# Attention and routed experts on one core: loads of q, k and v on ScalarE's queue, q without zero columns, first pair in halves, a new order

## Chip, cores, metric

One core of a Trainium2 chip. The metric is the device time of one execution in microseconds (us); lower is better. The engines are called as in the profile: PE (TensorE, matmuls; PEld its weight loads), DVE (VectorE), ACT (ScalarE), POOL (GpSimd) and SP (SyncE, which computes nothing and issues transfers).

## What is computed

```python
def rotate(x):
    x1, x2 = (x[..., :half], x[..., half:])
    return np.concatenate([x1 * cos - x2 * sin, x1 * sin + x2 * cos], axis=-1)
scores = scale * np.matmul(rotate(q), rotate(k).transpose(0, 1, 3, 2))   # q, k, v: (8, 8, 576, 64) float32
attn = np.exp(scores - np.max(scores, axis=-1, keepdims=True))
attn_out = np.matmul(attn / (np.sum(attn, axis=-1, keepdims=True) + 1e-9), v)
# x: attn_out with the 8 heads beside each other, (8, 576, 512)
scores = np.einsum('bsd,d->bs', x, w_gate)
out = x.copy()
for b in range(B):                       # 8 batches, capacity 128
    top_idx = np.argpartition(-scores[b], capacity)[:capacity]
    xe = x[b, top_idx]
    ye = np.maximum(xe @ w1, 0.0) @ w2   # w1 (512, 1024), w2 (1024, 512)
    g = 1.0 / (1.0 + np.exp(-scores[b, top_idx]))
    out[b, top_idx] = x[b, top_idx] + g[:, None] * ye
```

## The kernel before, in words

The work is cut into 32 pairs of heads, four pairs to a batch. The two heads of a pair lie on 64 partitions each. Each pair goes through these stages.

- **Load (`load`, lines 449 to 468).** One transfer each for k, q and v (lines 466 and 457), all issued by SP. The host lays k and q out with the two halves of the head dimension exchanged in a second copy, so k is 128 x 2 x 576 floats. q is 128 x 2 x 640: its last 64 columns stand twice, each time with zeros in the place of the other head, so that both heads' last rows can be one unit of matmuls (`_packed`, line 1060). k and q have one tile each, `k_in` and `q_in`; v has two, and a copy with exchanged partitions made by ACT or POOL (line 463).
- **Rotate (`rotate`, lines 470 to 506).** For k, then q: multiply by the tables of cosines and sines `tabs` (line 483), add the two copies into the one tile `turned` (line 485, one buffer for k and q alike), ACT casts the sum to the matmul's type (`kh`, `qh`, line 487), and the rest is subtracted out (`kl`, `ql`, line 488). POOL does the three element-wise steps for every pair but the first, DVE for the first.
- **Attend.** Nine units per pair (128 rows of one head; the ninth holds the last 64 rows of both). A unit: 3 products on PE (line 537: kh·qh, kl·qh, kh·ql), minimum and negation on DVE (line 558), exp on ACT (line 566), a transpose in blocks of 32 on DVE (line 589), a copy aside by ACT or POOL (line 595), transfers inside SBUF that put the halves in their places (`move`, line 621, `pt<-pt`, eight per pair; two of each four overwrite what the first two read and wait for them), and the product with v on PE (line 648). Then PE turns the rows (line 701) and ACT or DVE scales them (lines 716, 720).
- **Experts.** After four pairs SP stores the batch's rows, and `route` picks 128 of 576 rows by counting, gathers them, runs w1 and w2 on PE (line 925) and scatters them back. The weights come in 16 transfers with a cast on ACT and a subtraction on POOL (lines 987 to 991) during pairs 1 to 4.

**What sets the order.** Nothing is written out in program order. Every step is an `Op` with a key (a due time), the engines that could do it with their costs, and what it waits for. `Order.run` plays them through as a list schedule: a free engine takes the ready operation with the smallest key, and the instructions are emitted in that sequence, so each engine's stream (and SP's queue) has a fixed order that the planner believed good. `KEY` holds due times and thresholds, `SEEDS` draws small offsets for the keys, pair by pair. Urgent operations (units, softmax) may hold their engine idle up to `patience`; when PE has been less busy than `warm` of a stretch, the planner puts in idle matmuls (`L359`) that compute nothing. Transfers are planned on SP, one after the other: `moving` is the time at which the last one has passed, `size` how long each takes. The chip then runs the streams with semaphores; an engine that comes to an instruction too early waits there, and all behind it waits too.

**Start.** `tabs` is loaded whole by ACT (line 1002), then k, q and v of the first two pairs by SP.

Of the kernel before, what the change touches and what calls it, by code (L numbers as in the profile page):

```python
# [19 lines left out]
P = 128  # L20
# [3 lines left out]
KEY = dict(warm=0.72, warm0=20000, warm1=1000000, dummy=430, dcols=256, ahead=15000, lag=16000, rem=400, value=17500, rows=5250, load=29000, rotate=115700, half=2500,  # L24
           gate=10237, route=58400, count=31062, select=10850, turn=21875, step=7600, count_=20000, select_=3000, turn_=78750, step_=8550, last_step=1750, kstep=2700, hold=3,
           vcopy=6000, lift=range(9), lifted=688, patience=1400, over=600, near=-1050, swap=9750, vsplit=9, vstep=1500, recip=7500, pool_lo=1, esplit=1, t_most=4)


SEEDS = (287, 515, 547, 816, 264, 235, 869, 51, 137, 55, 51, 156, 400, 832, 65, 162, 511, 401, 998, 837, 195, 321, 307,
         523, 695, 769, 161, 691, 826, 584, 917, 834, 923)  # L30
# [14 lines left out]
class Order:  # L45
# [33 lines left out]
    def run(self):  # L79
# [23 lines left out]
        count, fetched, moving, landed = 0, 0.0, 0.0, []  # L103
# [35 lines left out]
        while events:  # L139
# [4 lines left out]
            while moved:  # L144
                moved = False
                for e in names:
# [3 lines left out]
                    while waiting[e]:  # L150
# [10 lines left out]
                        if can > t:  # L161
                            if o.urgent and can < t + KEY["patience"] and (soon is None or can < soon):
                                soon = can
                        elif soon is None or t + o.engines[e][0] <= soon + KEY["over"]:
# [109 lines left out]
def attention_moe_kernel(ctx: ExitStack, tc: tile.TileContext, q, k, v, gate, w1, w2, rope, outs, shape, cap):  # L274
# [43 lines left out]

    banks = ps.tile([P, 8, 512], F32, name="ps")
# [22 lines left out]

    T32, M512 = 109.0, 232.0
    LOAD, VALUES, WEIGHTS, STORE = {"SP": (600, 2100)}, {"SP": (600, 2050)}, {"SP": (520, 1400)}, {"SP": (600, 2200)}
# [23 lines left out]
    tabs = sb("tabs", [P, 2, REM + KW])  # L368
# [54 lines left out]
    nc.vector.memset(minus, -1.0)  # L423
    nc.gpsimd.iota(place, pattern=[[P, NT + 1]], base=0, channel_multiplier=1, allow_small_or_imprecise_dtypes=True)
# [21 lines left out]
    loaded, stacks = {}, {}  # L446
    last_first = []

    def load(pi, names="kqv", after=()):
# [3 lines left out]
        for i, (n, src, tiles) in enumerate((("k", k, k_ins), ("q", q, q_ins), ("v", v, vts))):  # L453
            if n in names:
                use = uses[n] = tiles.next()
                if n == "v":
                    o = op(VALUES, lambda src=src, use=use: nc.sync.dma_start(use.tile[:, 0], src[b, j]), key + i,
                           use.before + list(after), size=1050)
                    got[n].append(o)
                    for h in range(2):  # L460
                        mine, there = slice(64 * h, 64 * h + 64), slice(64 - 64 * h, 128 - 64 * h)
                        got[n].append(op({"ACT": act((NB // 2) * D), "POOL": pool_copy((NB // 2) * D)},
                                         lambda e, use=use, mine=mine, there=there: (nc.gpsimd.tensor_copy if e == "POOL" else nc.scalar.copy)(  # L463
                                             use.tile[mine, 1], use.tile[there, 0]), key + KEY["vcopy"], [o]))
                else:
                    got[n].append(op(LOAD, lambda src=src, use=use: nc.sync.dma_start(use.tile, src[b, j]), key + i,
                                     use.before + list(after), size=1900 if n == "k" else 2100))
                use.by(*got[n])

    def rotate(pi):  # L470
# [3 lines left out]
        key, base = at(pi, 0) - KEY["rotate"], at(pi, 0) - KEY["ahead"]  # L474
        kh, kl, qh, ql = (r.next() for r in (khs, kls, qhs, qls))
# [5 lines left out]
        def part(use, sum_use, sum_, tab, hu, lu, c0, c1, got):  # L481
            x, n = use.tile, c1 - c0
            m = op(time(2 * n), lambda: e.tensor_tensor(  # L483
                x[:, :, c0:c1], x[:, :, c0:c1], tab[:, :, c0:c1], op=ALU.mult), key, got)
            y = op(time(n), lambda: e.tensor_tensor(  # L485
                sum_[:, c0:c1], x[:, 0, c0:c1], x[:, 1, c0:c1], op=ALU.add), key, [m] + sum_use.before)
            c = op({"ACT": act(n)}, lambda: nc.scalar.copy(hu.tile[:, c0:c1], sum_[:, c0:c1]), base, [y] + hu.before)  # L487
            d = op(time(n), lambda: e.tensor_tensor(  # L488
                lu.tile[:, c0:c1], sum_[:, c0:c1], hu.tile[:, c0:c1].bitcast(F32), op=ALU.subtract), base, [c] + lu.before)
# [3 lines left out]
            return c0, c1, [c, d]  # L493

        for name, hu, lu in (("k", kh, kl), ("q", qh, ql)):
            use = uses[name]
            sum_use = turned.next()
            sum_ = sum_use.tile
            tab = tabs[:, :, 0:S] if name == "k" else tabs[:, :, REM:REM + KW]
            for c0, c1 in ((0, S),) if name == "k" else ((0, KW),) if not first else ((0, P), (P, MAIN), (MAIN, KW)):  # L500
                parts.setdefault(name, []).append(part(use, sum_use, sum_, tab, hu, lu, c0, c1, got[name] + wait))

# [619 lines left out]
```

## Time and profile before

| | us |
|---|---|
| median of 3 runs | 587.43 |
| lowest and highest | 586.22, 590.15 |
| profiled execution | 585.07 |
| its span, first to last instruction | 583.3 |

The profile is of one execution. Busy time is the time in which an engine executes; waits in an engine's own queue and the issue of a transfer by SP or ACT are not in it. A row of the timeline has start, duration, engine and line, what is written from what is read, the count, and in brackets how long the engine stood idle before it and what released it. A chain of waits is followed back from the last instruction to what released each step.

### The profile page before, as it was taken

Reading aid. Unit: us, or ns where it says so; the run is one execution under the profiler, and the core shown is the slowest. Engines: PE = TensorE matmul, PEld = TensorE weight load, DVE = VectorE, ACT = ScalarE, POOL = GpSimd, SP = SyncE. Lnnn points to the kernel's source line nnn. Section 1 sums busy time; section 2 is a strip of 40 time slices with the busy share of each in tenths; the row PEclk is TensorE's granted clock in tenths of the full one; section 3 lists DMA queues with packets and bytes.
Section 4 is the critical chain, followed back from the end, with each engine's and each line's share of the span. In section 5 each row is a group of like instructions: output and inputs, shape, how many; then the busy total and the mean of one; then the engine's idle time right before and its main releaser. Section 6 shows DMA issues by size and latency. Waiting matters only on the chain.

```text
span 583.3 us, 19385 instructions
## 1 busy us (share of the span) xinstructions
PE 523.4 (90%) x7496; PEld 434.2 (74%) x7496; DVE 495.5 (85%) x1242; ACT 477.9 (82%) x1318; POOL 452.9 (78%) x417
## 2 busy tenths in 40 slices
PE   0678889888998998999998999989889999899996
PEld 0567778677886887788877878778778778788884
DVE  6968989888989998999998998888899999899331
ACT  2759999988989988998887978898798988979321
POOL 3699999997999887897878888888799778924310
PEclk9979899998999999999999999999999999999999
DMA  5386888867787677868887677677878577645200
GB/s 216 106 236 185 241 264 231 252 179 238 197 246 197 194 215 191 219 178 220 246 198 203 157 214 195 194 196 199 238 212 224 147 217 200 181 111 136 72 31 24
DMA packets 55484, 110.83 MB, mean 190 GB/s; under 512 B 6752, under 2 KB 35808, under 8 KB 55392
## 3 DMA queue, kind: packets, MB, share of 16 engines
q1 hardware_dynamic: 53968, 104.67, 65.4%
q0 software_dynamic: 1280, 4.20, 2.2%
q8 instruction: 59, 0.97, 0.7%
q10 hardware_dynamic: 144, 0.72, 0.3%
q14 instruction: 33, 0.27, 0.1%
HBM read 56.30 MB, written 11.53 MB: 116 GB/s over the span
## 4 chain that ended last, share of the span: by engine, by line
DMA 28%; ACT 22%; POOL 17%; PE 10%; issue 10%; DVE 9%; SPq 2%; POOLq 0%; ACTq 0%; DVEq 0%
DMA pt<-pt 11%; ACT pab L566 8%; DMA q_in<-q_dram 7%; DMA vt<-v_dram 6%; ACT pt L595 4%; PE ps L648 4%; POOL turned L485 4%; POOL q_in L483 4%; DVE pt L589 4%; POOL k_in L483 3%; DVE pab L558 3%; PE ps L537 2%; ACT vt L463 2%; POOL kl L488 2%; PE ps L925 2%
## 5 line engine op out<-in xcount | busy, mean ns | idle before, releaser
L589 DVE STREAM_TRANSPOSE pt<-pab 128x576 f32<-128x576 f32 x256 | 190.3, 762 | 36.4 <-ACT pab L566 33.2
L566 ACT ACTIVATE pab<-pab,nm 128x576 f32<-128x576 f32 x256 | 196.5, 770 | 8.0 <-DVE pab L558 7.0
L558 DVE TENSOR_SCALAR_CACHE_REDUCE pab<-ps 128x576 f32<-128x576 f32 x256 | 180.6, 741 | 7.1 <-PE ps L537 6.1
L648 PE MATMUL ps<-pt,vt 64*64 64x128 f32 (+1 forms) x4608 | 159.3, 286 | 6.4 <-DVE pab L558 3.6
L648 PEld LDWEIGHTS ps<-pt,vt 64*64 64x64 f32 x4608 | 141.3, 133 | 18.9 <-issue 5.5
L537 PE MATMUL ps<-kh,qh 64*128 64x288 f32 (+1 forms) x576 | 90.0, 350 | 31.2 <-ACT qh L487 15.0
L483 POOL TENSOR_TENSOR q_in<-q_in,tabs 128x1280 f32<-128x1280 f32 x31 | 91.6, 2956 | 25.2 <-DMA q_in<-q_dram 23.2
L595 ACT COPY pt<-pt 128x288 f32<-128x288 f32 x227 | 89.9, 429 | 16.9 <-DMA pt<-pt 8.4
L537 PEld LDWEIGHTS ps<-kh,qh 64*128 64x128 f32 (+1 forms) x576 | 51.2, 189 | 69.4 <-ACT qh L487 15.4
L483 POOL TENSOR_TENSOR k_in<-k_in,tabs 128x1152 f32<-128x1152 f32 x31 | 82.7, 2667 | 10.6 <-DMA k_in<-k_dram 10.1
L537 PE MATMUL ps<-kh,ql 64*128 64x288 f32 (+1 forms) x576 | 71.8, 299 | 4.3 <-POOL ql L488 2.9
L537 PE MATMUL ps<-kl,qh 64*128 64x288 f32 (+1 forms) x576 | 71.1, 296 | 0.0
L701 PE MATMUL ps<-turner,ot 128*128 128x136 f32 x320 | 51.9, 294 | 8.3 <-ACT ot L348 5.4
L537 PEld LDWEIGHTS ps<-kh,ql 64*128 64x128 f32 (+1 forms) x576 | 54.2, 190 | 4.9 <-POOL ql L488 3.1
L701 PEld LDWEIGHTS ps<-turner,ot 128*128 128x128 f32 x320 | 43.0, 192 | 16.4 <-ACT ot L348 7.6
L537 PEld LDWEIGHTS ps<-kl,qh 64*128 64x128 f32 (+1 forms) x576 | 53.9, 190 | 0.0
L488 POOL TENSOR_TENSOR ql<-turned,qh 128x640 fp32r<-128x640 f32 x31 | 48.3, 1557 | 6.2 <-ACT qh L487 4.7
L925 PE MATMUL ps<-w,xt 128*128 128x512 f32 x192 | 52.9, 409 | 0.0
L925 PE MATMUL ps<-w,ht 128*128 128x512 f32 x192 | 51.1, 405 | 0.0
L485 POOL TENSOR_TENSOR turned<-q_in 128x640 f32<-128x640 f32 x31 | 48.3, 1558 | 1.2
L566 ACT ACTIVATION_READ_ACCUMULATOR pab<-pab,nm 128x1 f32 x256 | 48.2, 188 | 0.0
L488 POOL TENSOR_TENSOR kl<-turned,kh 128x576 fp32r<-128x576 f32 x31 | 44.1, 1423 | 2.4 <-ACT kh L487 2.1
(107 smaller groups left out, 738.6 us busy)
## 6 DMA issues: line engine op xcount, KB each, us to landing
pt<-pt SPq DMA_DIRECT2D x124, 180.0 KB, 4.4
q_in<-q_dram SPq DMA_DIRECT2D x32, 640.0 KB, 5.6
k_in<-k_dram SPq DMA_DIRECT2D x32, 576.0 KB, 6.0
pt<-pt SPq DMA_DIRECT2D x128, 144.0 KB, 3.8
vt<-v_dram SPq DMA_DIRECT2D x32, 288.0 KB, 4.1
out_dram<-x SPq DMA_DIRECT2D x16, 512.0 KB, 4.0
xe<-w_dram SPq DMA_DIRECT2D x8, 256.0 KB, 4.7
h<-w_dram SPq DMA_DIRECT2D x8, 256.0 KB, 5.4
```

Of the source, the lines that this page charges most:

```text
L463: lambda e, use=use, mine=mine, there=there: (nc.gpsimd.tensor_copy if e == "POOL" else nc.scalar.copy)(use.tile[mine, 1], use.tile[there, ...
L483: m = op(time(2 * n), lambda: e.tensor_tensor(x[:, :, c0:c1], x[:, :, c0:c1], tab[:, :, c0:c1], op=ALU.mult), key, got)
L485: y = op(time(n), lambda: e.tensor_tensor(sum_[:, c0:c1], x[:, 0, c0:c1], x[:, 1, c0:c1], op=ALU.add), key, [m] + sum_use.before)
L488: d = op(time(n), lambda: e.tensor_tensor(lu.tile[:, c0:c1], sum_[:, c0:c1], hu.tile[:, c0:c1].bitcast(F32), op=ALU.subtract), base, [c] + ...
L537: nc.tensor.matmul(bank_of(bs[i])[:, n, 0:HALF], lt, rt, start=start, stop=stop)
L558: nc.vector.tensor_scalar(halves, bank_of(b)[:, :, 0:HALF], -1.0, None, op0=ALU.mult, op1=ALU.min, accum_out=nm.tile[:, u:u + 1])
L566: lambda: nc.scalar.activation(halves, halves if lift else bank_of(b)[:, :, 0:HALF], AF.Exp, bias=nm.tile[:, u:u + 1], scale=-1.0 if lift ...
L589: nc.vector.transpose(into, src.rearrange("p (m w j) -> p m w j", w=2, j=32))
L595: (nc.gpsimd.tensor_copy if e == "POOL" else nc.scalar.copy)(apart(c)[:, to * L:to * L + L], two)
L648: nc.tensor.matmul(bank_of(acc)[64 * h:64 * h + 64, g, c0:c0 + 32 * n], vt.tile[gp_, h ^ g, (m - 1) % 2 * NT + (m - 1) // 2 if m else 2 * ...
L701: nc.tensor.matmul(bank_of(b)[:, W * i:W * i + W], ot.tile[:, i * P:i * P + P], turner, start=True, stop=True)
L925: nc.tensor.matmul(bank_of(bank), lhs.tile[:, a, c * P:c * P + P], w[w_][:, c, fs], start=(c == 0 and i == 0), stop=(c == n - 1 and i == 2))
```

## The change

- `KEY` and `SEEDS` get new values, so the whole order is another; `warm` goes from 0.72 to 0.86. Transfers are planned with other lengths, on two queues that slow each other when both move, and the moves count as urgent on SP.
- Loads of q, k and v from the second pair on, the gate and all loads of v are issued by ACT. Moves, stores and weights stay on SP.
- q is loaded as 128 x 2 x 576. The zeros stand in `q_sum` from the start; the sum of the last 64 columns is written by two more additions on 64 partitions each, between the zeros.
- `turned` becomes two tiles, `k_sum` and `q_sum`.
- For the first pair, k comes in two transfers of 288 columns, q in two of 128 and 448, the tables in three; the rotation follows in those pieces. The copy of the first v is due late and on ACT alone.

```diff
-KEY = dict(warm=0.72, ..., ahead=15000, lag=16000, value=17500, load=29000, rotate=115700,
-           route=58400, count=31062, select=10850, turn=21875, step=7600, count_=20000, turn_=78750, step_=8550, last_step=1750,
-           patience=1400, over=600, near=-1050, vstep=1500, ...)
+KEY = dict(warm=0.86, ..., ahead=15000, lag=16000, value=17500, load=30500, rotate=173549,
+           route=21900, count=23781, select=5425, turn=24609, step=11400, count_=24062, turn_=98437, step_=10820, last_step=4750,
+           patience=900, over=450, near=-900, vstep=2250, ..., ring="ACT", vring="ACT", wring="SP", issue=120,
+           svc0=800, svc1=200, svck=2101, svcq=2251, svcv=1501, first_moves=True, over_dma=750, patience_dma=1150)
...
-                    if e == "SP":
+                    if e == "SP" or e == "ACT" and o.size:
                         begin = max(begin, landed[-self.FLYING]) if len(landed) >= self.FLYING else begin
-                        moving = max(moving, begin + lasts) + o.size
-                        lasts = moving + self.LANDED - begin
+                        other = "ACT" if e == "SP" else "SP"
+                        from_ = max(moving[e], begin + lasts)
+                        both = min(o.size, max(0.0, moving[other] - from_))
+                        moving[e] = from_ + o.size + both
...
+    striped = lambda t: t[:, MAIN:KW].rearrange("p (a h j) -> p a h j", a=2, h=2)
+    ISSUE = {"SP": 420, "ACT": KEY["issue"]}
+    start_dma = lambda e: (nc.scalar if e == "ACT" else nc.sync).dma_start
-    LOAD, VALUES, ... = {"SP": (600, 2100)}, {"SP": (600, 2050)}, ...
+    LOAD, VALUES, ... = {KEY["ring"]: (ISSUE[KEY["ring"]], 1400)}, {KEY["vring"]: (ISSUE[KEY["vring"]], 1400)}, ...
...
-    q_ins = ring("q_in", 1, [P, 2, KW])
+    q_ins = ring("q_in", 1, [P, 2, S])
-    turned = ring("turned", 1, [P, KW])
+    k_sums = ring("k_sum", 1, [P, S])
+    q_sums = ring("q_sum", 1, [P, KW])
...
+    for h in range(2):
+        nc.vector.memset(striped(q_sums.tiles[0])[64 * h:64 * h + 64, :, 1 - h], 0.0)
...
+    FIRST = {"k": ((0, HALF), (HALF, S)), "q": ((0, P), (P, S))}
...
-                    got[n].append(op(LOAD, lambda src=src, use=use: nc.sync.dma_start(use.tile, src[b, j]), ...
+                elif pi:
+                    got[n].append(op(LOAD, lambda src=src, use=use: start_dma(KEY["ring"])(use.tile, src[b, j]), ...
+                else:
+                    for c, (c0, c1) in enumerate(FIRST[n]):
+                        got[n].append(op({"SP": (400, 1400)}, lambda ...: nc.sync.dma_start(
+                            use.tile[:, :, c0:c1], src[b, j, :, :, c0:c1]), ...
...
+            def add():
+                m1 = MAIN if edge else c1
+                e.tensor_tensor(sum_[:, c0:m1], x[:, 0, c0:m1], x[:, 1, c0:m1], op=ALU.add)
+                for h in range(2) if edge else ():
+                    hp = slice(64 * h, 64 * h + 64)
+                    a, b = (x[hp, i, MAIN:S].rearrange("p (a j) -> p a j", j=32) for i in range(2))
+                    e.tensor_tensor(striped(sum_)[hp, :, h], a, b, op=ALU.add)
...
-    nc.scalar.dma_start(tabs, rope)
+    cuts = (0, HALF, S, REM + S)
+    tabs_in = [op({"ACT": (400, 1400)}, lambda a=a, b=b: nc.scalar.dma_start(tabs[:, :, a:b], rope[:, :, a:b]), ...)
+               for i, (a, b) in enumerate(zip(cuts, cuts[1:]))]
...
-            load(pi + 1, "v")
+            load(pi + 1, "v", last_first[-1:] if not pi else ())
```

## Rows read from the trace of the kernel before

**Rows 1.** The page's chain that ended last, shares of the span by engine.
```profile
DMA 28%; ACT 22%; POOL 17%; PE 10%; issue 10%; DVE 9%; SPq 2%; POOLq 0%; ACTq 0%; DVEq 0%
```

**Rows 2.** By stretch: length, busy PE, PEld, DVE, ACT, POOL (instructions), clock, DMA share, GB/s.
```profile
0.00:35.00 35.00, 12.82 (x88) 10.59 (x90) 24.92 (x61) 15.78 (x35) 20.83 (x30) 0.94 0.52 171
35.00:100.00 65.00, 60.04 (x880) 49.77 (x877) 57.63 (x142) 61.32 (x167) 61.67 (x40) 0.95 0.82 231
...
535.00:583.00 48.00, 42.47 (x490) 35.99 (x486) 16.72 (x51) 15.02 (x43) 9.84 (x20) 0.97 0.20 61
35.00:535.00 500.00, 468.15 (x6928) 387.62 (x6928) 453.88 (x1132) 447.11 (x1242) 422.23 (x369) 0.99 0.75 204
```

**Rows 3.** Timeline of the first 35 us.
```profile
0.81 0.40 ACTq L1002 DMA_DIRECT2D tabs<-rope_dram  x1
...
0.81 0.38 SPq L466 DMA_DIRECT2D k_in<-k_dram  x1
...
1.25 0.42 SPq L466 DMA_DIRECT2D q_in<-q_dram  x1
...
1.71 1.07 SPq L457 DMA_DIRECT2D vt<-v_dram  x2
...
7.41 1.36 DVE L483 TENSOR_TENSOR k_in<-k_in,tabs 128x1152 f32<-128x1152 f32 x1 [4.29 <-DMA tabs<-rope_dram]
...
9.48 2.55 DVE L483 TENSOR_TENSOR q_in<-q_in,tabs 128x256 f32<-128x256 f32 x3
...
12.73 3.40 DVE L485 TENSOR_TENSOR turned<-q_in 128x384 f32<-128x384 f32 x3
...
17.55 0.76 DVE L558 TENSOR_SCALAR_CACHE_REDUCE pab<-ps 128x576 f32<-128x576 f32 x1 [0.54 <-PE ps L537]
...
20.14 2.94 POOL L483 TENSOR_TENSOR q_in<-q_in,tabs 128x1280 f32<-128x1280 f32 x1 [4.36 <-DMA q_in<-q_dram]
...
23.03 1.44 POOL L485 TENSOR_TENSOR turned<-k_in 128x576 f32<-128x576 f32 x1
...
34.11 0.76 DVE L558 TENSOR_SCALAR_CACHE_REDUCE pab<-ps 128x576 f32<-128x576 f32 x1 [3.64 <-PE ps L537]
```

**Rows 4.** Waits from 35 to 535: engine, line, released by: us, times, longest.
```profile
ACT vt L463 <- DMA vt<-v_dram: 10.6, 9, 1.9
ACT pt L595 <- DMA pt<-pt: 8.4, 7, 2.6
...
POOL q_in L483 <- DMA q_in<-q_dram: 18.8, 16, 2.7
...
POOL k_in L483 <- DMA k_in<-k_dram: 8.8, 8, 2.0
...
DVE pt L589 <- ACT pab L566: 33.2, 47, 2.0
```

**Rows 5.** Waits of SP's own queue, whole run: us, times, longest.
```profile
SPq L621 <- DMA pt<-pt: 102.2, 58, 5.7
SPq L466 <- POOL turned L485: 52.8, 26, 8.0
```

**Rows 6.** Issues of loads on SP: ns of one, minimum, median, maximum.
```profile
L466 SPq DMA_DIRECT2D q_in<-q_dram x32: 328/335/1424, 1.2 to 495.4; - x32
...
L457 SPq DMA_DIRECT2D vt<-v_dram x32: 323/526/1632, 1.7 to 521.6; - x32
```

**Rows 7.** Groups of instructions: count, busy us, mean ns, idle before.
```profile
L483 POOL TENSOR_TENSOR q_in<-q_in,tabs 128x1280 f32<-128x1280 f32 x31 | 91.6, 2956 | 25.2 <-DMA q_in<-q_dram 23.2 <-DMA vt<-v_dram 1.9
...
L483 POOL TENSOR_TENSOR k_in<-k_in,tabs 128x1152 f32<-128x1152 f32 x31 | 82.7, 2667 | 10.6 <-DMA k_in<-k_dram 10.1
...
L485 POOL TENSOR_TENSOR turned<-q_in 128x640 f32<-128x640 f32 x31 | 48.3, 1558 | 1.2
...
L359 PE MATMUL ps<-tabs,turner 128*128 128x256 f32 x128 | 35.7, 403 | 2.6 <-POOL pt L595 1.4 <-ACT gp L718 1.2
...
L786 POOL TENSOR_TENSOR gp<-gp,rs 128x40 f32<-128x40 f32 x7 | 1.9, 275 | 0.1
```

More of the change, by code (lines that the diff above doesn't have):

```diff
@@ L21 @@
 EPS = 1e-9
[L24 to L30, printed above, removed]
+KEY = dict(warm=0.86, warm0=20000, warm1=1000000, dummy=430, dcols=256, ahead=15000, lag=16000, rem=400, value=17500, rows=5250, load=30500, rotate=173549, half=2500,
+           gate=10237, route=21900, count=23781, select=5425, turn=24609, step=11400, count_=24062, select_=3000, turn_=98437, step_=10820, last_step=4750, kstep=2700, hold=3,
+           vcopy=6000, lift=range(9), lifted=688, patience=900, over=450, near=-900, swap=9750, vsplit=9, vstep=2250, recip=7500, pool_lo=1, esplit=1, t_most=4, ring="ACT", vring="ACT", wring="SP", issue=120, svc0=800, svc1=200, svck=2101, svcq=2251, svcv=1501, first_moves=True, over_dma=750, patience_dma=1150)
+SEEDS = (565, 391, 564, 144, 101, 455, 841, 8, 256, 824, 805, 812, 257, 897, 41, 772, 284, 205, 874, 236, 788, 528,
+         325, 737, 176, 896, 862, 855, 154, 898, 194, 459, 973)
 NOISE = 300.0
@@ L479, in rotate, with part @@
         parts = {}
-        def part(use, sum_use, sum_, tab, hu, lu, c0, c1, got):
+        def part(use, sum_use, sum_, tab, hu, lu, c0, c1, got, more=0):
             x, n = use.tile, c1 - c0
             m = op(time(2 * n), lambda: e.tensor_tensor(
[L484 to L487, printed above, removed]
+                x[:, :, c0:c1], x[:, :, c0:c1], tab[:, :, c0:c1], op=ALU.mult), key + more, got)
+            edge = name == "q" and c1 == S
+            def add():
[5 more added lines that the diff above has]
+                    e.tensor_tensor(striped(sum_)[hp, :, h], a, b, op=ALU.add)
+            y = op(time(n) if not edge else {"DVE": dve(n, 1, 200.0)} if first else {"POOL": pool(MAIN, 540.0)}, add, key + more, [m] + sum_use.before)
+            d1 = KW if edge else c1
+            n = d1 - c0
+            c = op({"ACT": act(n)}, lambda: nc.scalar.copy(hu.tile[:, c0:d1], sum_[:, c0:d1]), base + more, [y] + hu.before)
             d = op(time(n), lambda: e.tensor_tensor(
-                lu.tile[:, c0:c1], sum_[:, c0:c1], hu.tile[:, c0:c1].bitcast(F32), op=ALU.subtract), base, [c] + lu.before)
+                lu.tile[:, c0:d1], sum_[:, c0:d1], hu.tile[:, c0:d1].bitcast(F32), op=ALU.subtract), base + more + 3000 * first, [c] + lu.before)
             use.by(m, y), sum_use.by(y, c, d), hu.by(c, d), lu.by(d)
@@ L492, in part @@
                 last_first.append(y)
[L493 removed]
+            return c0, d1, [c, d]
+        whole = ((0, S),)
         for name, hu, lu in (("k", kh, kl), ("q", qh, ql)):
             use = uses[name]
[L497 removed]
+            sum_use = (k_sums if name == "k" else q_sums).next()
             sum_ = sum_use.tile
[L499 to L501 removed]
+            tab = tabs[:, :, 0:S] if name == "k" else tabs[:, :, REM:REM + S]
+            for i, (c0, c1) in enumerate(FIRST[name] if first else whole):
+                needs = [got[name][i]] + tabs_in[i if name == "k" else 0:i + 1 if name == "k" or not i else 3] if first else got[name] + wait
+                parts.setdefault(name, []).append(part(use, sum_use, sum_, tab, hu, lu, c0, c1, needs, first * (4000 * i + 2000 * (name == "q"))))
         def have(t):
[L504 removed]
+            return [o for x in parts["k"] for o in x[2]] + [o for c0, c1, l in parts["q"] if c0 <= t * P < c1 for o in l]
         stacks[pi] = (kh, kl, qh, ql, have)
@@ L1066, in _packed @@
     turned = x.reshape(B, H // 2, 2, S, D).transpose(0, 1, 2, 4, 3)
-    last = np.zeros((B, H // 2, 2, D, 2, 2, 32), x.dtype)
-    for h in range(2):
-        last[:, :, h, :, :, h] = turned[:, :, h][..., rest[:, 0]]
-    whole = [turned[..., rest.reshape(-1)], turned[..., main]]
-    if apart:
-        whole = [whole[1], last.reshape(B, H // 2, 2, D, -1)]
-    whole = np.concatenate(whole, -1)
+    whole = [turned[..., main], turned[..., rest]]
+    whole = np.concatenate(whole[::-1] if ahead else whole, -1)
     other = np.concatenate([whole[:, :, :, D // 2:], whole[:, :, :, :D // 2]], 3)
```

48 lines of the change are left out of this document (28 added, 20 removed).

## The prediction

> **What bounds the kernel now.** I read the chain that ended last first. No engine owns it: transfers have 28%, ACT 22%, POOL 17%, PE 10%, DVE 9% [rows 1]. The table by stretch says why. From 35 to 535 us, 500 us in which 31 pairs go by, PE is busy 468.15 us, DVE 453.88, ACT 447.11, POOL 422.23 [rows 2]. PE's figure flatters: 128 idle matmuls make 35.7 us of it [rows 7]. So three engines lie within a few per cent of each other, none is full, and the stage is bounded by DVE's 454 us at best: 46 us are lost to waits. The waits of that stage show DVE waiting 33.2 us for ACT's exp, ACT waiting 10.6 us for v and 8.4 for moved blocks, POOL waiting 18.8 us for q and 8.8 for k [rows 4]. Last I looked at SP's own queue, where those transfers come from: it stands 102.2 us in front of moves that wait for earlier moves, and 52.8 us in front of loads of k and q that wait for POOL to have read the old ones [rows 5]. A load that is ready stands behind such a move, and a move behind such a load.
>
> The ends are different. In the first 35 us DVE works 24.92, PE 12.82 and POOL 20.83 us [rows 2]. Nothing begins until the tables land at 7.41; the first softmax step is at 17.55; and DVE stands 3.64 us before the second pair goes on at 34.11, because POOL multiplied q only at 20.14 and added k only at 23.03 [rows 3]. The last 48 us are PE's, 42.47 busy, by the experts of the last batches [rows 2].
>
> **Start, in halves.** The first multiplication needs half of k and half of the tables. 704 KB of tables took from 0.81 to 7.41 beside k, q and v, the first loads of v being issued at 1.71 [rows 3]. By bytes alone half of k's columns, 288 of 704, would take 6.6 x 288/704 = 2.7 us. Whether landing goes by bytes no row shows, so the first step is 0 to 3.9 us earlier; I take 2.5, nearer the end that goes by bytes, since v now stands in ACT's stream behind the first casts and leaves the first microseconds to the others. Then DVE's path to the first unit: today k whole (1.36 for the product), q's three products 2.55, q's three sums 3.40 stand ahead of the first softmax [rows 3]. After it, of q only 128 of 640 columns must be done first: (2.55 + 3.40) x 512/640 = 4.8 us move behind it, less about 1 us in which the second half of k and of the tables is still landing. First softmax at about 17.55 - 2.5 - 3.8 = 11.3. The 4.8 us are not gone; DVE does them between units. What is gone is idle time: up to 4.29 us before 7.41 and the 3.64 before 34.11 [rows 3].
>
> For the second gap POOL's chain counts. With two sum tiles, q's sum no longer waits until k's low part is out of `turned`, and the second pair's loads no longer wait for all of the first q. From k's product to the last low part POOL needs 2.67 + 1.40 + 2.67 + 1.80 + 1.40 + 1.56 = 11.5 us (product and sum of k, the same of q, the two low parts; 576 columns as 1558 x 576/640 = 1.40, the 1.80 from below [rows 7]); begun at 12 to 13, when DVE has read the first k, it ends at 24 to 25. DVE's own work on the first pair (12.9 us from 17.55 to 34.11 - 3.64 = 30.47 [rows 3], plus the moved 4.8, all from 11.3 on) is then the later one and ends at 29. It needs 34.11 today. So 5 us, a little more with what DVE waits between its first steps today; bounds -2 (the first landing alone) and -8 (4.29 + 3.64). What it may run into: POOL is busy 61.67 of the next 65 us [rows 2], so POOL must have been released earlier too, which its own earlier start does. I take **-6**.
>
> **Loads issued by ACT.** 31 pairs by three loads. SP's issue of one takes 0.335 us for k or q and 0.526 for v in the median, 1.4 and 1.6 at most [rows 6]; ACT's one issue took 0.40 [rows 3]. If ACT can do nothing else meanwhile: 31 x (0.335 + 0.335 + 0.526) = 37 us, and ACT goes from 447 to 484 of 500 [rows 2], above DVE. If the issue runs beside an exp already started: 0. The nearest row is SP's own, but SP has no work that could cover it; ACT's waits (500 - 447 = 53 us) can. I take half as showing on ACT, 18 us, and of that ACT's share of the chain, 22% [rows 1]: **+4**, bounds 0 and +18 (484 us and the 53 - 19 = 34 us that ACT waits for other things than v and moves make 518 of today's 500). Behind a load on ACT stand the exps, and behind these DVE's transposes; the longest waits of that pair of engines already sum to 33.2 us [rows 4].
>
> The Trainium skill, "Advanced Engine Details and Errata", section "Sequencer and Instruction Queues", says that other engine instructions can be read and queued while a control instruction executes. By that the term would be 0 and the sum 4 us lower; no row here shows a load between two exps.
>
> **Waits for transfers.** With loads off SP's queue a move is held by moves alone, and a load by its buffer alone. Of the 46.6 us that ACT and POOL wait for transfers in the four largest rows (10.6 + 8.4 + 18.8 + 8.8 [rows 4]) not all can go, as the 16 engines are 75% busy in the stage and 82% in 35 to 100 [rows 2]. ACT's 19 us are nearly all on the path, POOL's 27.6 partly (it has 78 us to spare in 500). I let half of ACT's go (9.5) and a tenth of POOL's (2.8), less what comes late next, DVE, which has no more than 46 us above its own work: **-11**. Bounds 0 and -25. Two rings that move at once make each load longer; q's missing zeros give back 31 x 128 x 2 x 64 x 4 bytes = 2.0 MB, a tenth of q, which I count within this.
>
> A rule speaks against this term. The row first: from 35 to 100 us the transfer engines are 82% busy [rows 2]. "DMA: Bandwidth & Descriptors", section "Issuing engines are not separate DMA queues", of the Trainium skill says that transfers from several engines run on the same 16 engines and interleave, and that only the issue time is saved. The trace agrees in that one ring alone already reaches this share; by the rule the term is 0 (that is the second rival below).
>
> **POOL's arithmetic.** q's product shrinks from 2956 to 2667 ns [rows 7], 31 x 0.289 = -9.0 us of POOL. Its sum becomes 512 columns (1558 x 512/640 = 1.25) and two small additions, for which the nearest row is 275 ns [rows 7]: 1.80 against 1.558, +7.5 us. Net -1.5 us on an engine with 78 to spare: 0, between -1 and +2.
>
> **The rest.** More idle matmuls: each delays a real one by at most its 0.4 us [rows 7]; PE ran at a granted 0.94 and 0.95 in the first 100 us [rows 2], so some clock is won back. 0, between -3 and +3. Experts are due about two pairs earlier (route to turn sums to 75,700 against 122,200 planner ns at 20,000 a pair), which fills PE's idle gaps from 95 us on and can shorten the 48 us at the end or not: 0, between -4 and +4. The other seeds I count as noise, 0, between -5 and +5. The zeros of q's sum are two small memsets in DVE's 4.29 us wait [rows 3]: nothing, and as little if that cover goes.
>
> **Sum.** -6 + 4 - 11 + 0 = -13 on the profiled 585.07 gives 572. The profiled execution lies 2.4 us under the median of 587.43. From that median the sum gives 574.4. The terms overlap (a pair that starts earlier meets the same POOL, 61.67 of 65 us busy [rows 2]), so I take 2 off the gain: **576**.
>
> **Rivals.**
> *A, slower: ACT is held at the loads.* SP stands 52.8 us at loads of k and q, 26 times, 2.0 us each [rows 5]. On SP that costs nothing; on ACT the exps stand behind it. Where POOL is late against the planner's reckoning, the same wait falls on ACT. For it: half of 52.8 plus 18 us of issue makes ACT 447 + 44 = 491, and with its 19 us of transfer waits 510 in place of 500: +10, -6 at the start, no gain in waits, and some 5 us more that DVE waits for exps: 587.4 + 9 = 596. The stage grows from 16 us of such waits on, and from 22 us on they outweigh the start's gain. Against: the order is made anew, with the loads placed where the planner has the buffer free.
> *B, no change: the transfer waits only move.* Waits term 0, start and issue as above, -2 to 0: 585 to 587. For it: 75% busy transfer engines. Against: the 102.2 us of SP's queue.
> *C, much faster:* the issue is free and ACT's 19 us of waits go wholly, POOL's with them: 587.4 - 6 - 20 = 561. Against: DVE would stand at 95% of the stage.
> *D: the halves bring nothing*, since all pieces land together at 7.4. Then my forecast loses some 4 us: 580.
>
> **How the numbers follow.** Forecast with D inside it: 0.50, its own range 569 to 583. A 0.12, B 0.24, C 0.14. About 1% (5.9 us) is what a measurement of this kernel can tell from no change. Below 581.5 lie 0.46 of the forecast's 0.50, all of C and 0.04 of B: 0.64. Above 593.3 lies most of A: 0.10. The rest, 0.26, is within 1%. For 8 in 10 the range goes down to 563, which takes in the half of C that falls a little short, and up past B to 590; A and the rest of C, some 0.18, stay out.
>
> **What would show it.** Right: DVE's first step near 5 us, first softmax near 11, second pair's near 28; POOL's waits at q and k smaller by a third or more; the sum of ACT's waits for v and moves about halved; ACT's idle time before an exp no longer for a load's release. Wrong: exps that wait with a load issue between them (A); the same sums of waits under other names with a transfer share near 0.8 (B); POOL between 35 and 100 above 62 of 65 us with the start's gain gone by 100 us.

## The result and the profile after

The change made the kernel slower by about 1%: the ratio of after to before is 1.0115 [1.0083, 1.0148], the median of after 594.70 us against 586.73 us for before, each of 20 runs. Forecast were 576 and a range of 563 to 590. Six of after's 20 runs, the profiled one of 599.67 us (span 598.0) among them, fell in a slower state and count in the median but not in the ratio, so sums of waits in that profile may be some us high.

Line numbers of the changed kernel: units L570, minimum L591, exp L599, transpose L622, copy aside L628, moves L654, product with v L681, end of a pair L719, rotation L504 and L510/L514, casts L519, loads of k and q L481, of v L469, idle matmuls L367.

**The start.** Timeline of after, the rows that answer to [rows 3]:

```profile
5.46 0.76 DVE L504 TENSOR_TENSOR k_in<-k_in,tabs 128x576 f32<-128x576 f32 x1 [2.01 <-DMA k_in<-k_dram]
...
10.15 1.08 DVE L504 TENSOR_TENSOR q_in<-q_in,tabs 128x896 f32<-128x896 f32 x1
...
11.26 0.56 DVE L510 TENSOR_TENSOR q_sum<-q_in 128x384 f32<-128x384 f32 x1
11.74 0.45 DVE L514 TENSOR_TENSOR q_sum<-q_in 64x64 f32<-64x64 f32 x2
12.22 0.76 DVE L591 TENSOR_SCALAR_CACHE_REDUCE pab<-ps 128x576 f32<-128x576 f32 x1
12.22 0.62 ACT L519 CAST qh<-q_sum 128x512 fp32r<-128x512 f32 x1 [1.10 <-DVE q_sum L514]
12.23 0.33 ACTq L469 DMA_DIRECT2D vt<-v_dram  x1
...
12.82 2.65 POOL L504 TENSOR_TENSOR k_in<-k_in,tabs 128x1152 f32<-128x1152 f32 x1 [10.39 <-DMA k_in<-k_dram]
...
13.69 2.32 DVE L520 TENSOR_TENSOR ql<-q_sum,qh 128x512 fp32r<-128x512 f32 x1
...
18.55 0.78 ACT L599 ACTIVATE pab<-pab,nm 128x576 f32<-128x576 f32 x1
...
18.74 0.33 ACTq L481 DMA_DIRECT2D k_in<-k_dram  x1
...
29.32 0.76 DVE L591 TENSOR_SCALAR_CACHE_REDUCE pab<-ps 128x576 f32<-128x576 f32 x1 [0.54 <-PE ps L570]
```

DVE's first step is at 5.46 (7.41 before), the first softmax at 12.22 (17.55), the second pair's, behind the nine units of the first, at 29.32 (34.11). Loads of v and k are issued by ACT's queue at 12.23 and 18.74, while ACT's cast of 12.22 and its exp of 18.55 run. Of the 94 loads of k, q and v that ACT issues in this profile, 67 have ACT at work beside them for more than nine tenths of the issue.

**Where the gain of the start goes.** The end of a pair is its sum of rows on DVE (L686 before, L719 after). Timeline of before, pairs 2, 5 and 32:

```profile
49.70 0.17 DVE L686 TENSOR_REDUCE rs<-sums 128x10 f32<-128x20 f32 x1
...
96.00 0.17 DVE L686 TENSOR_REDUCE rs<-sums 128x10 f32<-128x20 f32 x1
...
538.43 0.13 DVE L686 TENSOR_REDUCE rs<-sums 128x10 f32<-128x20 f32 x1
```

The same three pairs in the timeline of after:

```profile
45.53 0.13 DVE L719 TENSOR_REDUCE rs<-sums 128x10 f32<-128x20 f32 x1
...
96.63 0.16 DVE L719 TENSOR_REDUCE rs<-sums 128x10 f32<-128x20 f32 x1
...
555.25 0.13 DVE L719 TENSOR_REDUCE rs<-sums 128x10 f32<-128x20 f32 x1
```

After is 4.2 us ahead at pair 2, 0.6 behind at pair 5, 16.8 behind at the last. The loss lies in the stage of pairs. The tail behind the last pair got shorter: 598.0 - 555.25 = 42.8 us against 583.3 - 538.43 = 44.9.

**The stage.** By stretch, after, with the columns of [rows 2] (length, busy PE, PEld, DVE, ACT and POOL, clock, share of the transfer engines, GB/s):

```profile
35.00:535.00 500.00, 473.47 (x6783) 392.00 (x6779) 440.06 (x1115) 413.34 (x1110) 422.32 (x449) 0.97 0.71 195
```

Waits from 35 to 535 us, with the columns of [rows 4]: two of before that do not stand there, then those of after.

```profile
ACT pab L566 <- DVE pab L558: 5.8, 16, 1.1
...
DVE pab L558 <- PE ps L537: 1.9, 5, 1.0
```

```profile
ACT pab L599 <- DVE pab L591: 20.4, 26, 4.8
...
DVE pab L591 <- PE ps L570: 16.9, 21, 3.1
DVE pt L622 <- ACT pab L599: 14.0, 29, 1.3
ACT pt L628 <- DMA pt<-pt: 9.6, 8, 3.7
...
ACT w L1022 <- DMA xe<-w_dram: 6.5, 3, 2.4
...
POOL q_in L504 <- DMA q_in<-q_dram: 3.3, 3, 2.1
```

The waits for loads fell: POOL's for q from 18.8 [rows 4] to 3.3 us, ACT's for v from 10.6 [rows 4] to nothing that this list shows. ACT's waits for all transfers together did not: their sum over the list is about 21 us before and 24 after, as those for the experts' weights (`w`) rose from 1.8 to 9.8. No engine but PE (by its idle matmuls) became busier: DVE does 440 us in these 500 where it did 454 [rows 2], ACT 413 where it did 447. The largest new waits are those of the computing engines for each other. Exp's wait for the minimum was 5.8 us before and is 20.4; the minimum's for PE was 1.9 and is 16.9; only the transpose's wait for exp fell, 33.2 [rows 4] to 14.0: 40.9 us of the three became 51.3.

**SP's queue**, whole run, after, as [rows 5]:

```profile
SPq L654 <- DMA pt<-pt: 166.1, 81, 6.1
SPq L654 <- ACT pt L628: 108.5, 37, 16.8
```

With the loads gone SP stands 166.1 us before moves that wait for moves (102.2 [rows 5]), and 108.5 us for ACT's copies (40.1 before): SP comes to each move earlier and stands there instead. This idleness costs nothing by itself.

**Groups**, after, as [rows 7]:

```profile
L504 POOL TENSOR_TENSOR q_in<-q_in,tabs 128x1152 f32<-128x1152 f32 x31 | 82.9, 2674 | 3.5 <-DMA q_in<-q_dram 3.3
...
L510 POOL TENSOR_TENSOR q_sum<-q_in 128x512 f32<-128x512 f32 x31 | 39.9, 1286 | 0.7
...
L514 POOL TENSOR_TENSOR q_sum<-q_in 64x64 f32<-64x64 f32 x62 | 19.7, 318 | 8.9 <-DMA xe<-out_dram,idx 6.8
...
L367 PE MATMUL ps<-tabs,turner 128*128 128x256 f32 x212 | 60.3, 407 | 4.5 <-ACT gp L751 3.1 <-DVE pab L591 1.1
```

POOL has for q 2.674 + 1.286 + 2 x 0.318 = 4.60 us a pair where it had 2.956 + 1.558 = 4.51 [rows 7]. Idle matmuls are 212, before 128.

**A hold at a load.** The worst place of after, timeline from 436.85 us:

```profile
436.85 0.61 ACT L973 ACTIVATE h<-ps 128x512 f32<-128x512 f32 x1
...
439.95 0.33 ACTq L469 DMA_DIRECT2D vt<-v_dram  x1
440.32 0.70 ACT L356 COPY ot<-ps 128x256 f32<-128x256 f32 x3 [2.87 <-DMA pt<-pt]
...
441.08 0.85 PE L570 MATMUL ps<-kh,qh 128*128 128x288 f32 x2 [2.92 <-ACT ot L356]
...
441.67 0.69 DVE L984 TENSOR_TENSOR ht<-ps,ht 128x512 fp32r<-128x512 f32 x1 [3.41 <-ACT ht L981]
```

ACT has nothing running from 437.46 on (436.85 + 0.61); the load in its stream waits until 439.95, the copy behind it starts at 440.32, PE then at 441.08 and DVE at 441.67: three engines stand about 3 us for one load. The bracket puts ACT's 2.87 us down to the landing of a move, but the copy reads PE's result and nothing that a move writes: it is the load ahead of it that waited. By the trace's semaphores PE had left the load's buffer at the latest 1.77 us before the issue; what came last, 0.08 us before it, was the landing of a transfer that shares the load's completion semaphore (last section). The columns of [rows 2] for these stretches:

```profile
438.00:442.00 4.00, 1.08 (x6) 0.92 (x5) 0.59 (x3) 1.63 (x5) 4.00 (x3) 0.75 0.77 182
442.00:446.00 4.00, 4.00 (x26) 3.47 (x29) 1.82 (x4) 3.96 (x11) 1.67 (x3) 0.50 0.60 150
```

In the 4 us behind the hold PE was granted 0.50, the lower of its two levels (1.2 of 2.4 GHz), and was busy all the time, where it had worked 1.08 of the 4 us before: PE pays the hold a second time. In the whole profile of after, ACT had run out of work more than 0.15 us before a load could be issued in 13 places, 11.7 us in sum (the first table load, at 0.81 with nothing ahead of it, is no hold).

### The profile page after: what moved, and what is told of

Its sections match the earlier page's. It is cut to its first block, busy times and chain, and to the rows that moved or that the text cites. A ratio compares the mean times of both kernels' runs of the same rounds, so it can differ in the third digit from the quotient of the medians.

```text
span 598.0 us, 19685 instructions
## 1 busy us (share of the span) xinstructions
PE 550.7 (92%) x7580; PEld 455.1 (76%) x7580; DVE 497.4 (83%) x1261; ACT 465.3 (78%) x1254; POOL 462.0 (77%) x516
## 5 line engine op out<-in xcount | busy, mean ns | idle before, releaser
L599 ACT ACTIVATE pab<-pab,nm 128x576 f32<-128x576 f32 x256 | 196.7, 771 | 22.4 <-DVE pab L591 21.0
L622 DVE STREAM_TRANSPOSE pt<-pab 128x576 f32<-128x576 f32 x256 | 189.3, 760 | 17.1 <-ACT pab L599 15.2
L591 DVE TENSOR_SCALAR_CACHE_REDUCE pab<-ps 128x576 f32<-128x576 f32 x256 | 181.4, 744 | 19.7 <-PE ps L570 17.7
L681 PE MATMUL ps<-pt,vt 64*64 64x128 f32 (+1 forms) x4608 | 161.3, 291 | 0.4 <-ACT pt L639 0.2
L681 PEld LDWEIGHTS ps<-pt,vt 64*64 64x64 f32 x4608 | 144.1, 137 | 12.3 <-issue 5.1
L570 PE MATMUL ps<-kh,qh 64*128 64x288 f32 (+1 forms) x576 | 91.4, 355 | 23.6 <-ACT qh L519 9.7
L628 ACT COPY pt<-pt 128x288 f32<-128x288 f32 x215 | 85.7, 429 | 21.9 <-DVE pt L622 10.7
L570 PEld LDWEIGHTS ps<-kh,qh 64*128 64x128 f32 (+1 forms) x576 | 51.4, 192 | 63.2 <-issue 18.6
L504 POOL TENSOR_TENSOR k_in<-k_in,tabs 128x1152 f32<-128x1152 f32 x31 | 82.8, 2671 | 13.1 <-DMA k_in<-k_dram 11.9
L504 POOL TENSOR_TENSOR q_in<-q_in,tabs 128x1152 f32<-128x1152 f32 x31 | 82.9, 2674 | 3.5 <-DMA q_in<-q_dram 3.3
L570 PE MATMUL ps<-kh,ql 64*128 64x288 f32 (+1 forms) x576 | 72.1, 300 | 3.3 <-DVE ql L520 1.8
L570 PE MATMUL ps<-kl,qh 64*128 64x288 f32 (+1 forms) x576 | 71.6, 299 | 0.0
L367 PE MATMUL ps<-tabs,turner 128*128 128x256 f32 x212 | 60.3, 407 | 4.5 <-ACT gp L751 3.1
L570 PEld LDWEIGHTS ps<-kh,ql 64*128 64x128 f32 (+1 forms) x576 | 54.6, 193 | 3.9 <-DVE ql L520 2.2
L520 POOL TENSOR_TENSOR ql<-q_sum,qh 128x640 fp32r<-128x640 f32 x31 | 48.5, 1565 | 10.4 <-ACT qh L519 7.9
L570 PEld LDWEIGHTS ps<-kl,qh 64*128 64x128 f32 (+1 forms) x576 | 54.6, 192 | 0.0
L734 PEld LDWEIGHTS ps<-turner,ot 128*128 128x128 f32 x320 | 44.5, 194 | 7.0 <-issue 2.7
L367 PEld LDWEIGHTS ps<-tabs,turner 128*128 128x128 f32 x212 | 38.0, 198 | 13.9 <-ACT gp L751 3.5
L599 ACT ACTIVATION_READ_ACCUMULATOR pab<-pab,nm 128x1 f32 x256 | 48.5, 189 | 0.0
```

What stands on the lines that cost most here:

```text
L367: nc.tensor.matmul(bank_of(b)[:, 0:KEY["dcols"]], ident, tabs[:, 0, 0:KEY["dcols"]], start=True, stop=True)
L504: m = op(time(2 * n), lambda: e.tensor_tensor(x[:, :, c0:c1], x[:, :, c0:c1], tab[:, :, c0:c1], op=ALU.mult), key + more, got)
L520: d = op(time(n), lambda: e.tensor_tensor(lu.tile[:, c0:d1], sum_[:, c0:d1], hu.tile[:, c0:d1].bitcast(F32), op=ALU.subtract), base + more ...
L570: nc.tensor.matmul(bank_of(bs[i])[:, n, 0:HALF], lt, rt, start=start, stop=stop)
L591: nc.vector.tensor_scalar(halves, bank_of(b)[:, :, 0:HALF], -1.0, None, op0=ALU.mult, op1=ALU.min, accum_out=nm.tile[:, u:u + 1])
L599: lambda: nc.scalar.activation(halves, halves if lift else bank_of(b)[:, :, 0:HALF], AF.Exp, bias=nm.tile[:, u:u + 1], scale=-1.0 if lift ...
```

## The experiments

Three explanations stood against each other: ACT is held at the loads; the added idle matmuls stand in the way; the new order itself is worse, whatever issues the loads. All ratios are to the kernel before on the same chip, with a 95% interval; the changed kernel stands at 1.0115. Times beside them are medians of all runs.

**Idle matmuls.** In the old order each is issued twice (256):

```diff
-            nc.tensor.matmul(bank_of(b)[:, 0:KEY["dcols"]], ident, tabs[:, 0, 0:KEY["dcols"]], start=True, stop=True)
+            for _ in range(2):
+                nc.tensor.matmul(bank_of(b)[:, 0:KEY["dcols"]], ident, tabs[:, 0, 0:KEY["dcols"]], start=True, stop=True)
```

> The kernel before with every idle matmul issued twice (256 in place of 128), nothing else moved. Theory I (the loss is PE's: 84 more idle matmuls stand in front of real work): 128 more at some 0.24 us each are 30 us of PE, half of it in the way, so 8 to 20 us slower than before. Theory L (the loss comes from loads held in ACT's stream) and theory O (the loss is the new order itself): within 4 us of before, as PE was waiting where they stand.

1.0016 [0.9988, 1.0045], 589.53 us: no price in the old order that can be told. In the changed kernel two of five are left out (127 stay; they compute nothing that is used):

```diff
+        if o.fn.__name__ == "dummy":
+            idles += 1
+            if idles % 5 in (1, 3):
+                continue
```

> The changed kernel with two of each five idle matmuls left out where they stood (127 in place of 212), the order otherwise the same. Theory I: 6 to 12 us faster than the changed kernel, about the kernel before. Theories L and O: within 3 us of the changed kernel, or slower where PE's clock falls more often.

1.0178 [1.0134, 1.0222], 597.44 us, slower than the changed kernel: the added ones are not the loss. Doubled in the changed kernel (424), with the edit of the first:

> The changed kernel with every idle matmul issued twice (424). If a fallen clock is part of the loss: 2 to 6 us faster than the changed kernel, as fewer of them made it some 4 us slower. If the number does not matter beyond chance: within 2 us. If they stand in the way: 3 to 15 us slower.

1.0407 [1.0355, 1.0459], 611.84 us. Group of the idle matmuls, and waits from 35 to 535 us, of this run:

```profile
L368 PE MATMUL ps<-tabs,turner 128*128 128x256 f32 x424 | 103.4, 388 | 0.0
```

```profile
ACT pab L600 <- DVE pab L592: 31.2, 32, 6.1
DVE pab L592 <- PE ps L571: 27.5, 39, 2.9
```

The clock was 0.992 in this profile (0.971 in after's), and 43 us more of idle matmuls than after's 60.3 made minimum wait for PE 27.5 us instead of 16.9. So neither fewer nor more would mend the changed kernel; the same doubling is free in one order and costs 2.9% in the other.

**Loads back on SP, in the new order.** All of them, at the same places of the order:

```diff
-    start_dma = lambda e: (nc.scalar if e == "ACT" else nc.sync).dma_start
+    start_dma = lambda e: nc.sync.dma_start
```

> The changed kernel, same order, but the loads of q, k, v, the gate are issued by SP at the place in the order where ACT issued them. Theory L: ACT idles 14 us in front of loads in the changed kernel; without them 5 to 10 us faster than the changed kernel. Theory I: within 2 us of the changed kernel. If the second queue is worth what the prediction said (moves no longer behind loads): 8 to 15 us slower than the changed kernel.

1.0033 [1.0002, 1.0064], 589.94 us. Against after that is 1.0115/1.0033 = 1.008, some 4.8 us that ACT as issuer costs. Then v alone (line 469 issues with `nc.sync`):

> The changed kernel, same order, loads of v alone issued by SP, k and q still by ACT. In the changed kernel ACT idles longest in front of loads of v (2.86, 1.94, 1.72 us). If v carries the price: 4 to 5 us faster than the changed kernel, the whole of what all loads on SP gave back. If k and q carry it, waiting for POOL: within 1.5 us of the changed kernel.

0.9979 [0.9948, 1.0010], 586.10 us: 1.4% or 8 us better than after. Then k and q alone (line 481 with `nc.sync`):

> The changed kernel, same order, loads of k and q issued by SP, v still by ACT. If v carries the price: within 1.5 us of the changed kernel. If k and q carry it: 4 to 5 us faster. If each load has its share: about half in each of the two runs.

1.0044 [1.0005, 1.0082], 592.48 us: 0.7% or 4 us better than after. The end of pair 5 with v on SP, from its timeline, beside 96.63 in after and 96.00 in before:

```profile
93.78 0.16 DVE L719 TENSOR_REDUCE rs<-sums 128x10 f32<-128x20 f32 x1
```

With v on SP the start's gain still stands there (2.2 us), and ACT is held in only 4 places, 1.5 us in all where after has 13 and 11.7. The parts don't add: taking v alone from ACT gives 8 us, k and q alone 4, all three 5.

**Loads on ACT, in the old order.** From the second pair on:

```diff
-                    o = op(VALUES, lambda src=src, use=use: nc.sync.dma_start(use.tile[:, 0], src[b, j]), key + i,
+                    o = op(VALUES, lambda src=src, use=use: (nc.scalar if pi else nc.sync).dma_start(use.tile[:, 0], src[b, j]), key + i,
...
-                    got[n].append(op(LOAD, lambda src=src, use=use: nc.sync.dma_start(use.tile, src[b, j]), key + i,
+                    got[n].append(op(LOAD, lambda src=src, use=use: (nc.scalar if pi else nc.sync).dma_start(use.tile, src[b, j]), key + i,
```

> The kernel before, same order, but from the second pair on its loads of q, k and v are issued by ACT where SP issued them. Theory L: ACT stands at loads as SP did (52.8 us in front of k and q), so 10 to 30 us slower than before. The prediction's view (issue half hidden, transfers wait less): between 7 us faster and 4 us slower. Theory I says nothing of it.

1.0063 [1.0030, 1.0095], 591.76 us, with 10 holds of ACT, 9.0 us in sum. It is about the price of the new order (0.8%), the other way round. Waits from 35 to 535 us of this run (its profiled execution took 597.52 us):

```profile
DVE pab L558 <- PE ps L537: 14.2, 12, 3.7
POOL q_in L483 <- DMA q_in<-q_dram: 12.4, 11, 1.8
...
ACT vt L463 <- DMA vt<-v_dram: 5.3, 6, 1.4
POOL k_in L483 <- DMA k_in<-k_dram: 4.8, 5, 1.8
```

The waits for loads fell by 15.7 us (18.8, 10.6 and 8.8 before [rows 4]), as the second queue was to do, and the time rose: the minimum now waits 14.2 us for PE where it waited 1.9. Only k and q (the second of the two edits):

> The kernel before, same order, k and q issued by ACT from the second pair on, v left on SP. Theory V (the price of ACT's loads is v's, which waits for PE and for a move): 0 to 6 us faster than before, where all three on ACT were 3.7 us slower. Theory L for all loads alike: 1 to 4 us slower than before.

1.0367 [1.0315, 1.0420], 607.66 us, far above the 0.6% of all three loads together, though ACT is held at 2 loads alone, 0.8 us: holds are not the only price. Waits from 35 to 535 us of this run, then SP's own queue:

```profile
DVE pt L589 <- ACT pab L566: 44.5, 42, 4.9
ACT vt L463 <- DMA vt<-v_dram: 22.4, 13, 4.8
```

```profile
SPq L457 <- PE ps L648: 27.8, 15, 4.3
```

v is late: ACT waits 22.4 us for it (10.6 [rows 4]), and the exps behind that copy make DVE wait 44.5 (33.2 [rows 4]). SP now comes to v before its buffer is free and stands there 27.8 us (7.6 before). Why v also lands later for it was not settled.

**v later in ACT's stream**, so that ACT isn't held at it: from the third pair on each load of v is emitted four ACT instructions later, at the latest ahead of its first copy.

```diff
+        if late.get(id(o)):
+            kept.append([4, o, e])
+            continue
+        for x in [x for x in kept if o in x[1].outs or x[0] == 0]:
+            emit(*x[1:])
+            kept.remove(x)
```

> The changed kernel with each load of v from the third pair on issued four ACT instructions later in ACT's stream (never behind the first copy that reads it), all else in the same order. If ACT standing in front of v's loads is the price: 4 to 8 us faster than the changed kernel, near the run with v on SP (0.998 of before). If it is the time at which v moves: within 2 us of the changed kernel, or slower as v's copies wait.

1.0510 [1.0464, 1.0557], 618.22 us. Waits of this run from 35 to 535 us:

```profile
ACT vt L477 <- DMA vt<-v_dram: 35.9, 17, 6.4
```

The holds at v went (6 at k and q are left, 4.3 us in sum), and 35.9 us of waiting for v came. The load of v has hardly any room: early it holds ACT, late ACT waits for it.

**The order itself.** The planner draws small offsets for its keys from `SEEDS`. Both kernels with other draws and nothing else changed: without offsets, and with 7, 13 or 29 added to each seed.

```diff
-NOISE = 300.0
+NOISE = 0.0
```

```diff
-    draws = [random.Random(1000 * i + n) for i, n in enumerate(SEEDS)]
+    draws = [random.Random(1000 * i + n + 7) for i, n in enumerate(SEEDS)]
```

Without offsets, the old kernel and the new one:

> The kernel before with the small drawn offsets of the due times at zero, so that the order is drawn up anew from the same keys. If an order is worth no more than chance: within 6 us of before either way. If the old draws were a good hand: 6 to 20 us slower.

> The changed kernel with the drawn offsets at zero. Theory O (the new order costs some 6 us after the first pairs): if by its draws alone, this run is as likely faster as slower than the changed kernel, within 8 us; if by its keys and its model of transfers, it is slower than the kernel before with zero offsets by some 5 us or more.

With +7:

> The kernel before with other random offsets of the same size on its due times. Theory H (the old kernel's draws are a chosen hand, worth some 26 us over none): 10 to 30 us slower than before. If only the absence of offsets was bad: within 8 us of before.

> The changed kernel with other random offsets. Theory H: between 595 and 608, thus faster than the kernel before with other offsets by 5 to 20 us, as it was by 2.4% with none. If the change is worse in itself: slower than that run or equal to it.

With +13:

> The kernel before with a third set of random offsets. Theory H (its own set is a chosen hand, an unchosen one costs 2 to 4.5%): 1.5 to 5% slower than before. Theory C (the change is worse in itself): the same here, but below the changed kernel with the same set.

> The changed kernel with that third set. Theory H: 1.5 to 5% slower than the kernel before, on either side of the run above. Theory C: more than 1% slower than the run above.

With +29:

> The kernel before with a fourth set. Theory H: 1.5 to 5% slower than before.

> The changed kernel with that fourth set. Theory H: on either side of the run above, and over the four sets (none, and three) the means of both kernels within 1% of each other. Theory C: slower than the run above by 1% or more, as in at least three of the four.

| draws | kernel before | kernel after |
|---|---|---|
| as given | 1 | 1.0115 [1.0083, 1.0148] |
| none | 1.0443 [1.0403, 1.0483] | 1.0200 [1.0146, 1.0253] |
| +7 | 1.0196 [1.0152, 1.0239] | 1.0461 [1.0407, 1.0516] |
| +13 | 1.0107 [1.0037, 1.0177] | 1.0267 [1.0173, 1.0361] |
| +29 | 1.0265 [1.0168, 1.0363] | 1.0235 [1.0136, 1.0333] |

Every other order is slower than its kernel's own, by 1.1 to 4.4% in the old kernel and 0.8 to 3.4% in the new one (1.0461/1.0115). That looks as if the draws of both kernels had been picked; that they were is not shown. The other orders average 1.025 before and 1.029 after; they scatter by 1.4 and 1.2% (standard deviation), so the means differ by 0.4% with a standard error of 0.9%. With four draws each, the change apart from its draws has no sign that can be told; a gain of 2% (the forecast) would be two and a half such errors away. How the loss shows with the draws +7 in the new kernel, waits from 35 to 535 us:

```profile
ACT pab L599 <- DVE pab L591: 26.3, 25, 6.8
...
DVE pab L591 <- PE ps L570: 23.2, 22, 7.1
```

The same waits as in after, each longer.

**Two parts that pay without the rest.** The old order and start, loads on SP, q without zero columns and with two sum tiles:

```diff
-    q_ins = ring("q_in", 1, [P, 2, KW])
+    q_ins = ring("q_in", 1, [P, 2, S])
...
-    turned = ring("turned", 1, [P, KW])
+    turned = ring("q_sum", 1, [P, KW])
+    k_sum = sb("k_sum", [P, S])
...
+                for h in range(2) if c1 == KW else ():
+                    hp = slice(64 * h, 64 * h + 64)
+                    a, b = (x[hp, i, MAIN:S].rearrange("p (a j) -> p a j", j=32) for i in range(2))
+                    e.tensor_tensor(striped(sum_)[hp, :, h], a, b, op=ALU.add)
```

> The kernel before, same order, q loaded and multiplied without the zero columns, the sums of k and q in two tiles; loads stay on SP, the start is as it was. The prediction counted this at nothing, between 1 us slower and 2 us faster for POOL's arithmetic, with less to transfer; with the second tile 1 to 5 us faster than before. If the small additions cost POOL more than the product gives back: slower by 1 to 3 us.

0.9949 [0.9913, 0.9986], 584.26 us, the one version clearly faster than both kernels. Its wait for q from 35 to 535 us:

```profile
POOL q_in L487 <- DMA q_in<-q_dram: 11.5, 12, 2.4
```

POOL waits 7 us less for q (18.8 [rows 4]), which agrees with a shorter q on a queue in the old order. What the second sum tile has of it was not told apart.

## Why the prediction was wrong, point by point

- **What bounds the kernel: right, and not followed through.** Three engines within a few per cent and 46 us of waits was what the rows said. As I read it now, each wait in the stage is set by the fixed order of five streams. I treated the waits as terms that can be taken off one by one.
- **The step that failed: waits for transfers, -11.** "I let half of ACT's go (9.5) and a tenth of POOL's (2.8)". POOL's waits for q fell by 15.5 us and for k by 7.3 (8.8 [rows 4] to 1.5), ACT's for v by 10.6, and nothing of it reached the end. ACT's waits for all transfers rose, from about 21 to 24 us; its wait for moves did not fall (8.4 to 9.6). Between the engines, exp's wait for the minimum grew by 14.6 and the minimum's for PE by 15.0 us. What the second queue is worth is shown by the runs that change the issuer alone: the loads on ACT cost 4.8 us in the new order and 3.7 (0.63%) in the old, where this term and the issue's +4 gave -7. That is 11 to 12 of the roughly 18 us between 0.981 (576 of 587.43) and 1.0115. B (the waits only move) had the mechanism, though not for its reason: the transfer engines were less busy, 71% against 75% [rows 2].
- **Issue by ACT, +4 (half shown):** no price seen. Issues of 0.33 us stand beside a running cast or exp (12.23, 18.74), and the run with 62 loads of k and q left on ACT stands at 0.9979. The trace agrees with the rule weighed there, "Advanced Engine Details and Errata", section "Sequencer and Instruction Queues", of the Trainium skill. What I put on the rival A, the hold, came in its stead.
- **Start, -6:** -4.2 at the end of pair 2, and it is real. The first softmax came at 12.22, forecast 11.3, the second pair's at 29.32, forecast near 28, but not in the way worked out: all of q was multiplied and added ahead of the first. What I moved behind it as 4.8 us (a share of the 2.55 and 3.40 [rows 3]) takes 1.08 + 0.56 + 0.45 = 2.1 us in after, most likely because POOL is idle until 12.82 (the last section). D, that the halves bring nothing, fell: the first step is 1.95 us earlier.
- **The other seeds, 0, between -5 and +5, and the order made anew:** the bounds were too narrow for one order. The other draws put the old kernel 6 to 26 us above its own time, all to one side, and the new one 5 to 20. But what the exchange of one set of draws for the other cost is not told: the two kernels differ by 1.15% with their own draws and by 0.4% over the others, and the 0.75% between these, some 4 us, is within the error of 0.9% and within the bounds.
- **What is left, some 6 us.** With all loads on SP the new order stands at 1.0033, 2 us above before, where the start and the overlap (-6 + 2) alone gave -4. It keeps the start's gain up to pair 5 and loses it behind (timeline of that run, pairs 5 and 32, beside 96.00 and 538.43 of before):

```profile
93.66 0.16 DVE L719 TENSOR_REDUCE rs<-sums 128x10 f32<-128x20 f32 x1
...
545.74 0.12 DVE L719 TENSOR_REDUCE rs<-sums 128x10 f32<-128x20 f32 x1
```

- **POOL's arithmetic, 0:** 4.60 against 4.51 us a pair, +0.08; right. Idle matmuls and experts, 0: the tail is 2.1 us shorter, the matmuls are not the loss.
- **A, slower by ACT's holds:** it gave 596, and 594.7 came; the nearness is in part luck. Its mechanism was there at less than half its size (11.7 us of holds, not 26), and the 5 us more that DVE was to wait for exps did not come: that wait fell from 33.2 [rows 4] to 14.0.

Shown is: the loads on ACT cost (two orders, both directions); the idle matmuls are not the cause; other draws move either kernel by 1 to 4%. How much of that cost is the hold is only argued: with k and q alone on ACT in the old order it was largest with almost no holds, and v, issued later, was late. Why after's order in particular is 0.3% slower than the old one with the same issuer is open.

## What to carry to other kernels

Where several engines are each about 90% busy in fixed streams, the sum of a kind of wait is no price: before taking it off, ask which engine stands next in its place. A single order of such a kernel can stand several per cent from its neighbours (here 1 to 4%); a change that makes the order anew must be judged by several draws of both kernels, and the parts that leave the order alone (here q without zeros with two sum tiles, 0.5%, and the issuer, 0.6%) should be timed alone first. A load in a computing engine's stream was issued for nothing here while the engine ran, but its wait held everything behind it, so put there only loads whose buffers and completion semaphores are free long before, and time it.

## What the runs showed of the hardware that I had not expected

**DVE, adding two inputs, stands while POOL works.** In the run without zero columns, timeline of the start:

```profile
12.93 2.72 POOL L487 TENSOR_TENSOR k_in<-k_in,tabs 128x1152 f32<-128x1152 f32 x1 [1.51 <-DVE q_sum L493]
12.95 2.78 DVE L497 TENSOR_TENSOR q_sum<-q_in 64x64 f32<-64x64 f32 x2
```

Two additions of 64 columns took DVE 2.78 us, as long as POOL's product that began beside them; in after, with POOL idle, the same two took 0.45 us. One of the three sums of 3.40 us [rows 3] had 2.73 us of it in the same way: POOL's product ran from 13.09 to 15.78. "SBUF — State Buffer", section "SBUF: two separate sides", of the Trainium skill says that VectorE with two inputs from SBUF and a GpSimd instruction that reads SBUF take a shared port for a whole instruction, and that the later one is blocked. The trace agrees. After is not free of it: its low part of q, behind the first softmax, took 2.32 us from 13.69 on, beside POOL's product of 12.82. A DVE duration taken beside a busy POOL is no price for the same step elsewhere.

**Transfers of two queues share their completion semaphores.** In the built program all transfers that SP and ACT issue take eight completion semaphores in turn, in the order in which they are emitted, so a load on ACT may also wait for the transfer eight before it, in about half of these cases a move of SP's. Of ACT's loads 19 of 31 for k, 23 of 31 for q and 26 of 32 for v carry such a wait. From ACT's stream (line, transfer, what it waits for beside its engine's own order):

```
L481 DMA q_in_75<-q_dram 128x1152 [waits DMAHW2_49]
...
L469 DMA vt_88<-v_dram 128x576 [waits DMAHW3_49,PE_49]
```

So a load held "by its buffer alone", as I put it, is the exception here: two queues still hold each other. In after 3 of the 13 holds ended with such a landing, the two longest among them (2.49 and 1.57 us up to the issue), and 10 with POOL's or PE's release of the buffer. In these three the buffer was free earlier: without the shared semaphores at least 3.5 of the 11.7 us would have gone. That is an estimate from the times of the semaphores; what it would save at the end is open.
